# State sums copied by ScalarE, and rank and table products queued behind column transposes or state reads, in an attention and top-1 expert kernel

## Chip, cores and metric

The kernel runs on one core of one Trainium2 chip. The metric is the time of one execution on the device in microseconds (us); the number for a kernel is the median of several runs. Three runs of the kernel before gave 663.51, 663.2 and 663.98 us.

## What is computed

The reference is attention in both directions between tokens and states, followed by a layer of experts in which each row goes to one expert. Cut to what matters:

```python
# x: 8 batches, 8 heads, 512 tokens, 64;  state: 8, 8, 32, 64
scores = x @ state.T / 8                    # per batch and head
xread  = softmax(scores) @ state            # token reads, over the 32 states
sread  = softmax(scores.T) @ x              # state reads, over the 512 tokens
x = concat([xread, sread], axis=2) -> rows  # 8 * (512 + 32) = 4352 rows of 512
e_idx = argmax(x @ w_gate)                  # one of 8 experts for each row
out[row] = gate_w * sigmoid(x @ w_output_gate)[e] * (relu(x @ w1[e]) @ w2[e])
```

## The kernel before

The program has two stages. The first, some 185 us, is the attention and the routing; the second runs the experts in units of two or three tiles of 128 rows, under an order written by hand. The change lies wholly in the first stage, in whose code the order on each engine is set by a scheduler: it takes instructions in the order in which they are written, as far as their inputs and buffers are expected to be ready.

The first stage loops over the eight batches b (lines 468 to 499). What matters of one step, with its lines:

- `x_trans(b+1)`: TensorE transposes x (line 325), ScalarE copies to SBUF (327).
- `e2_trans(b)`: transposes of the column exponentials (424), copied by ScalarE (426).
- `scores(b+1)`: products (337), scaled by ScalarE into `s_sb` (340). VectorE takes the row maximum (344), subtracts it (346), ScalarE takes exp (347), VectorE sums and inverts (348 to 350), GpSimd multiplies (351).
- `a_trans(b)`: transposes of the row softmax of b (359); ScalarE writes the high half `aThi` (362), VectorE the low half `aTlo` (363).
- `columns_softmax(b+1)`: eight transposes of `s_sb` (401, the "column transposes"), VectorE's maximum (403), ScalarE's exp (406), VectorE's sum and inverse (407, 408).
- `state_reads(b)`: products of x and the column softmax into the single buffer `pss` (436, the "state reads"), and two copies of 64 by 256 out of it into `srT` (440, the "state sums").
- `token_reads(b)`: four groups px0 to px3 of six products each (380 to 382; 382 reads `aTlo`), each copied out by ScalarE (383).
- `state_out(b)` after b = 3 and b = 7: products of `srT` with the gate weights (449), read by VectorE (453 to 455).
- For GpSimd there are also the split of state values (205 to 210), the split of expert weights (496, 497), and small copies (415).

Routing runs beside this in generators that `go_on` advances. A route finds each row's expert (227 to 235 on VectorE), ranks the rows of each expert by products with a triangular matrix (243 to 247, the "rank products", also in `pss`), turns ranks to places (252 to 286), and builds for each chunk of 128 rows a pair `pa`, `rb` (294, 296), whose product is added to the table of row numbers `tid_ps` (300, the "table products"). `pa` has three buffers, and the scratch tile `lgp` of line 453 takes one of the same three.

Four limits set the order: TensorE, VectorE, ScalarE and GpSimd each execute their own list strictly as it stands; all large results of TensorE share three PSUM buffers named `psb` (transposes, scores, px groups, `state_out`); `pss` has one buffer; and each buffer is free only when its last reader is done.

After the loop, the rest of the routing ends in a chain of small VectorE operations and table products, twelve warm-up products (line 138, called at 503), the gathers of the first unit (614), its transposes (625), and the first expert products (655).

## Time and profile before

| what | value |
|---|---|
| runs of the kernel before | 663.51 us median, 663.2 to 663.98 |
| profiled execution | 662.72 us, span 661.0 us |
| TensorE matmul busy | 615.7 us, 93% of the span |
| VectorE, ScalarE, GpSimd busy | 283.8, 235.3, 181.8 us |
| first expert product starts | 188.91 us |
| mean granted TensorE clock | 0.968 |

The span is from the first to the last instruction; 1.72 us of the execution's time lie outside it. In a row of the timeline stand the start, the duration, the engine (PE is TensorE, DVE VectorE, ACT ScalarE, POOL GpSimd), the line of the kernel, the operation, output and inputs, the number of instructions merged and, in brackets, how long the engine sat idle before and whom that wait is put down to. The view of windows gives for each stretch its length, then for PE, PE's weight loads, DVE, ACT and POOL the busy time with the number of instructions, then the granted clock (1.00 is full), the share of the DMA engines and GB/s. A TensorE product of 32-bit data with 64 columns of output shows as two instructions.

### The profile page before, as it was taken

To read this page: it belongs to the slowest core of one execution; us is meant where nothing else is said; L and a number is where in the kernel's file an instruction comes from. 1 tells how busy PE (TensorE), PEld (TensorE's weight loads), DVE (VectorE), ACT (ScalarE), POOL (GpSimd) and SP (SyncE) were. 2 spreads that over 40 slices of the span, in tenths; PEclk is the share of its full clock that TensorE was granted. 3 is DMA by queue.
4 is the path that set the end of the run, shared out by engine and by line. 5 is a ranking of instruction groups with operands and counts; after the bars stand their busy time and mean duration, and the time that the engine had idled before them with its cause. 6 is when DMAs were issued, how large, how long until landed. Compare 5 with 4: busy or idle time off the path is not lost. (4 is left out here: it accounts for less than half of the span.)

```text
span 661.0 us, 11440 instructions
## 1 busy us (share of the span) xinstructions
PE 615.7 (93%) x3941; PEld 551.6 (83%) x3941; DVE 283.8 (43%) x626; ACT 235.3 (36%) x391; POOL 181.8 (27%) x286
## 2 busy tenths in 40 slices
PE   7989979998689999999999999999999999999990
PEld 4888978897468998998989989898898998988980
DVE  5547797878863211221235243154123424363210
ACT  3455534445042222222334244244233424462210
POOL 8154562641041221121122203124111220322210
PEclk8989998999679999999999999999999999999996
DMA  8533442323175220220146224325314522475200
GB/s 221 213 123 101 152 160 63 129 68 116 35 244 178 67 82 19 66 84 33 51 161 193 83 93 171 124 83 199 141 51 161 193 82 83 150 266 194 67 34 19
DMA packets 46288, 78.56 MB, mean 119 GB/s; under 512 B 11056, under 2 KB 19248, under 8 KB 46192
## 3 DMA queue, kind: packets, MB, share of 16 engines
q1 hardware_dynamic: 38592, 52.00, 24.1%
q0 software_dynamic: 7600, 25.38, 11.4%
q8 instruction: 49, 0.80, 0.5%
q14 instruction: 47, 0.39, 0.2%
HBM read 101.98 MB, written 19.42 MB: 184 GB/s over the span
## 5 line engine op out<-in xcount | busy, mean ns | idle before, releaser
L662 DVE SCALAR_TENSOR_TENSOR hlo<-p,hhi 128x256 fp32r<-128x256 f32 (+1 forms) x136 | 62.1, 462 | 226.9 <-ACT hhi L661 214.6
L655 PE MATMUL p<-xhi,whi 128*128 128x256 f32 (+1 forms) x544 | 151.2, 301 | 1.2 <-ACT xhi L627 0.8
L656 PE MATMUL p<-xhi,wlo 128*128 128x256 f32 (+1 forms) x544 | 150.1, 298 | 1.5 <-issue 1.5
L688 POOL DMA_INDIRECT out_dram<-y,idx x38 | 39.5, 1040 | 319.7 <-ACT y L687 236.0
L681 PE MATMUL po<-whi,hhi 128*128 128x512 f32 x304 | 122.6, 403 | 0.0
L682 PE MATMUL po<-wlo,hhi 128*128 128x512 f32 x304 | 120.1, 395 | 0.0
L655 PEld LDWEIGHTS p<-xhi,whi 128*128 128x128 f32 x544 | 103.6, 191 | 2.3 <-ACT rest_of L671 1.1
L661 ACT ACTIVATE hhi<-p 128x256 fp32r<-128x256 f32 (+1 forms) x136 | 56.5, 417 | 137.6 <-PE p L658 134.6
L656 PEld LDWEIGHTS p<-xhi,wlo 128*128 128x128 f32 x544 | 103.5, 190 | 1.9 <-issue 1.7
L658 PE MATMUL p<-xlo,whi 128*128 128x256 f32 (+1 forms) x544 | 95.9, 298 | 0.0
L685 PE MATMUL po<-whi,hlo 128*128 128x512 f32 x304 | 83.2, 395 | 0.0
L658 PEld LDWEIGHTS p<-xlo,whi 128*128 128x128 f32 x544 | 81.1, 190 | 0.0
L614 POOL DMA_INDIRECT xg<-xa,idx x57 | 66.2, 1161 | 48.7 <-issue 17.1
L687 ACT ACTIVATE y<-po,xg 128x512 f32<-128x512 f32 x38 | 26.2, 689 | 132.7 <-PE po L685 49.7
L685 PEld LDWEIGHTS po<-whi,hlo 128*128 128x128 f32 x304 | 57.0, 187 | 14.0
L682 PEld LDWEIGHTS po<-wlo,hhi 128*128 128x128 f32 x304 | 57.2, 188 | 11.6
L681 PEld LDWEIGHTS po<-whi,hhi 128*128 128x128 f32 x304 | 57.1, 188 | 11.5
L642 DVE TENSOR_TENSOR wlo<-stage,whi 128x2048 fp32r<-128x2048 f32 x24 | 54.3, 2285 | 11.6 <-ACT whi L635 11.6
L628 DVE TENSOR_TENSOR xlo<-pxT,xhi 128x512 fp32r<-128x512 f32 x39 | 25.9, 687 | 62.7 <-ACT xhi L627 62.7
L635 ACT CAST whi<-stage 128x2048 fp32r<-128x2048 f32 x24 | 45.1, 1901 | 3.8 <-DVE hlo L662 1.7
L627 ACT CAST xhi<-pxT 128x512 fp32r<-128x512 f32 x39 | 22.2, 583 | 30.7 <-PE pxT L625 30.7
L436 PE MATMUL pss<-e2T,xb 128*128 128x64 f32 x256 | 29.9, 275 | 1.1 <-ACT e2T L426 1.1
(190 smaller groups left out, 726.1 us busy)
## 6 DMA issues: line engine op xcount, KB each, us to landing
stage<-in_moe_w_dram SPq DMA_DIRECT2D x74, 1024.0 KB
xb<-in_x_dram SPq DMA_DIRECT2D x7, 1024.0 KB
xa<-xm SPq DMA_DIRECT2D x7, 1024.0 KB
xb<-in_x_dram SPq DMA_DIRECT2D x2, 512.0 KB
xa<-xm SPq DMA_DIRECT2D x4, 256.0 KB
xg<-xa,idx POOLq DMA_INDIRECT x57, 3.6
out_dram<-y,idx POOLq DMA_INDIRECT x38, 3.1
sraw<-in_state_dram SPq DMA_DIRECT2D x2, 256.0 KB
```

Source lines behind the costliest of these rows:

```text
L614: g = nc.gpsimd.indirect_dma_start(out=xg_all[u % 3][i], out_offset=None, in_=xa[:, :], in_offset=bass.IndirectOffsetOnAxis(ap=ix, axis=0))
L635: nc.scalar.copy(whi[i], stage[i])
L642: nc.vector.tensor_sub(wlo[i], stage[i], whi[i].bitcast(F32))
L655: nc.tensor.matmul(p1[:, :n], lhsT=whi[i][:, k, c], rhs=hi[:, k, :n], start=(k == 0), stop=False)
L656: nc.tensor.matmul(p1[:, :n], lhsT=wlo[i][:, k, c], rhs=hi[:, k, :n], start=False, stop=False)
L658: nc.tensor.matmul(p1[:, :n], lhsT=whi[i][:, k, c], rhs=lo[:, k, :n], start=False, stop=(k == KX - 1))
L661: nc.scalar.activation(hhi[:, fb, :n], p1[:, :n], AF.Relu)
L662: nc.vector.scalar_tensor_tensor(hlo[:, fb, :n], in0=p1[:, :n], scalar=0.0, in1=hhi[:, fb, :n].bitcast(F32), op0=ALU.max, op1=ALU.subtract)
L681: nc.tensor.matmul(po, lhsT=hhi[:, f, c], rhs=whi[j][:, k, :], start=(f == 0), stop=False)
L682: nc.tensor.matmul(po, lhsT=hhi[:, f, c], rhs=wlo[j][:, k, :], start=False, stop=False)
L685: nc.tensor.matmul(po, lhsT=hlo[:, f, c], rhs=whi[j][:, k, :], start=False, stop=(f == KH - 1))
L688: nc.gpsimd.indirect_dma_start(out=out[:, :], out_offset=bass.IndirectOffsetOnAxis(ap=idx[:, W * u + t : W * u + t + 1], axis=0), in_=y, i ...
```

## The change

Two things are changed. The two copies of the state sums (440) are issued on ScalarE instead of VectorE. And two kinds of products get an ordering edge, without a semaphore, to the latest column transpose or state read on the same engine (`st["pe"]`): the first rank product of a route, unless it is one of the last, and each table product while fewer than NT - 9 = 25 are done. Such an edge only tells the scheduler that the product may not stand before that instruction in TensorE's list.

```diff
+    def behind(inst, before):
+        tc.add_manual_dep(inst.ins, before.ins.name, mybir.DependencyInfo(mybir.DependencyClass.NoSync, mybir.DependencyReason.DATA), reason="order")
...
-            nc.tensor.matmul(rkv, lhsT=tri, rhs=ohb, start=True, stop=False)
+            m = nc.tensor.matmul(rkv, lhsT=tri, rhs=ohb, start=True, stop=False)
+            if len(done) < NT - 5:
+                behind(m, st["pe"])
...
                     done.append(nc.tensor.matmul(tid_ps, lhsT=pa, rhs=rb, ...
+                    if len(done) < NT - 9:
+                        behind(done[-1], st["pe"])
...
-                    nc.tensor.transpose(tp[:, g, P * c : P * c + P], s_v[:, c, g, :], ident)
+                    st["pe"] = nc.tensor.transpose(tp[:, g, P * c : P * c + P], s_v[:, c, g, :], ident)
...
-                    nc.tensor.matmul(srv[:, h], lhsT=xb[:, h, 2 * cc : 2 * cc + 2, :]...
+                    m = nc.tensor.matmul(srv[:, h], lhsT=xb[:, h, 2 * cc : 2 * cc + 2, :]...
+            st["pe"] = m
...
-                nc.vector.tensor_copy(srT[D * k : D * k + D, :, NS * bb : NS * bb + NS], srv[D * k : D * k + D, :, k, :])
+                nc.scalar.copy(srT[D * k : D * k + D, :, NS * bb : NS * bb + NS], srv[D * k : D * k + D, :, k, :])
```

The scheduler's lists differ at three kinds of places. Line numbers in the changed file are higher by 4 to 9: its 449 is the copy of line 440, 391 is 383, 355 is 347, 409 is 401, 247 to 253 are 243 to 247, and 371 is 363.

ScalarE at b = 2 (b = 6 reads alike), first before, then changed. `s_sb` are scores, `a_sb` the row exponentials, `e` the column exponentials, `xm` the copies of px groups:

```order
L340 ACTIVATE s_sb<-psb 128x1024
L362 CAST aThi<-psb 128x1024
L347 ACTIVATE a_sb<-a_sb 128x1024
L383 COPY xm<-psb 128x544
L406 ACTIVATE e_790,st_788<-psb,st_788 128x512 x2
```

```order
L348 ACTIVATE s_sb<-psb 128x1024
L370 CAST aThi<-psb 128x1024
L449 COPY srT<-pss 64x8x32 x2
L355 ACTIVATE a_sb<-a_sb 128x1024
L391 COPY xm<-psb 128x544
L414 ACTIVATE e_790,st_788<-psb,st_788 128x512 x2
```

The copies stand between the high half and the row exponential, so the exponential, the px copies and the column exponential queue behind the state reads.

VectorE from b = 3 to b = 4, first before, then changed (`lgp` and `xs` are what `state_out` reads from PSUM, `st_1184` the row statistics of the next scores):

```order
L294 TENSOR_SCALAR pa<-iota_q,rf_1004 128x128
L296 TENSOR_SCALAR rb<-iota_q,sm_861,vid 128x272
L453 TENSOR_TENSOR lgp<-psb,rs 128x128
L455 TENSOR_TENSOR xs<-psb,rs 128x512
L454 TENSOR_REDUCE lgt<-lgp 128x16
L294 TENSOR_SCALAR pa<-iota_q,rf_1004 128x128
L227 TENSOR_REDUCE sm_1106<-lgt 128x1
```

```order
L302 TENSOR_SCALAR rb<-iota_q,sm_861,vid 128x272
L352 TENSOR_REDUCE st_1184<-s_sb 128x32
L371 TENSOR_TENSOR aTlo<-psb,aThi 128x1024
L462 TENSOR_TENSOR lgp<-psb,rs 128x128
L464 TENSOR_TENSOR xs<-psb,rs 128x512
L463 TENSOR_REDUCE lgt<-lgp 128x16
L354 TENSOR_TENSOR a_sb<-s_sb,st_1184 128x1024
L231 TENSOR_REDUCE sm_1106<-lgt 128x1
```

The three reads of `state_out` moved behind the next batch's row maximum and low half: the table products that free `lgp`'s buffer are now held behind the column transposes.

TensorE at b = 1 (b = 3 and b = 5 are of the same kind), first before, then changed:

```order
L245 MATMUL pss<-ohb_477,ones 128x8
L247 LDWEIGHTS ones
L247 MATMUL pss<-run_bf,ones 128x32
L401 MATMUL psb<-ident,s_sb 128x128 x8
L380 MATMUL psb<-sbd_181,aThi 128x272
L381 MATMUL psb<-sbd_182,aThi 128x272
```

```order
L367 MATMUL psb<-ident,a_sb 128x128 x8
L409 MATMUL psb<-ident,s_sb 128x128 x8
L247 LDWEIGHTS tri
L247 MATMUL pss<-ohb_477,tri 128x32
L251 LDWEIGHTS ones
```

The rank products moved from ahead of the column transposes to behind them. At b = 2 and b = 6 two table products moved in the same way, and two state reads stand in their place. At b = 7 the changed list has the rank products ahead of all token reads, where before they stood among them, and VectorE makes their input ahead of the low half, not behind it. On GpSimd two small value splits (209, 210) moved ahead of a multiplication; on SyncE the small write of line 458 moved ahead of the last load of x, and one row write of b = 7 behind two factor writes.

## Prediction

> **What bounds the kernel now.** I read the page, then the timeline of each engine from 28 us to 200 us, then the view of windows. A change within 0.2% of the run, some 1.3 us, is about what a measurement of this kernel cannot tell from none.

> ```profile
> span 661.0 us, 11440 instructions
> ...
> PE 615.7 (93%) x3941; PEld 551.6 (83%) x3941; DVE 283.8 (43%) x626; ACT 235.3 (36%) x391; POOL 181.8 (27%) x286
> ```

> TensorE bounds the kernel. Its work is the same after the change, so time can come only from its idle stretches in the attention stage and from its clock. For the clock I cut the timeline where the granted clock jumps, and the jumps lie on a grid of 3.41 us:

> ```profile
> 37.79:41.20 3.41, 1.07 (x7) 0.85 (x8) 2.90 (x5) 1.45 (x4) 1.91 (x1) 1.00 0.74 244
> 41.20:44.61 3.41, 3.41 (x18) 3.41 (x17) 0.13 (x1) 1.74 (x3) 0.72 (x4) 0.50 0.01 3
> 95.83:99.24 3.41, 1.34 (x13) 1.23 (x12) 3.35 (x8) 0.00 (x0) 3.15 (x8) 1.00 1.01 302
> 99.24:102.65 3.41, 3.41 (x19) 3.41 (x18) 2.90 (x3) 0.25 (x1) 3.27 (x5) 0.50 0.78 213
> 157.24:160.65 3.41, 2.14 (x22) 1.84 (x22) 3.04 (x13) 0.77 (x2) 0.00 (x0) 1.00 0.26 94
> 167.48:170.89 3.41, 1.69 (x20) 1.59 (x18) 2.43 (x11) 0.00 (x0) 0.00 (x0) 1.00 0.01 2
> 187.96:191.37 3.41, 2.66 (x13) 2.47 (x12) 2.62 (x11) 2.49 (x2) 0.00 (x0) 0.50 0.84 308
> 191.37:194.78 3.41, 3.41 (x18) 3.41 (x17) 0.42 (x1) 0.73 (x2) 2.72 (x3) 0.50 1.06 392
> 194.78:198.20 3.42, 3.42 (x31) 3.42 (x30) 3.01 (x3) 2.15 (x4) 2.81 (x3) 1.00 0.73 234
> ```

> A window with PE busy 1.07 or 1.34 us is followed by one at half clock. So idle time is charged twice: as itself, and as a window at half speed. Between 50% busy (1.69 us) and 63% (2.14 us, and I found no half clock behind it) lies the threshold. Back to full clock 78% (2.66) was not enough, 100% was.

> The idle stretch of b = 0 is the first that the copies of line 440 make:

> ```profile
> 35.41 0.86 DVE L440 COPY srT<-pss 64x256 f32<-64x256 f32 x2 [2.00 <-PE pss L436]
> 36.45 1.04 PE L401 MATMUL psb<-ident,s_sb 128*128 128x128 f32 x8
> 38.16 1.23 DVE L403 TENSOR_REDUCE st<-psb 128x2 f32<-128x1024 f32 x1
> 39.30 1.22 DVE L363 TENSOR_TENSOR aTlo<-psb,aThi 128x1024 fp32r<-128x1024 f32 x1
> 40.57 0.40 PE L382 MATMUL psb<-sbd,aTlo 128*128 128x272 f32 x1 [2.34 <-DVE aTlo L363]
> ```

> **The change part by part. The copies at b = 0.** VectorE waited 2.00 us for the state reads, with line 348 queued behind the copies. Without them line 348 starts 2 us earlier and line 403 waits only for the transposes, done at 36.45 + 1.04 = 37.49: it starts at 37.55 instead of 38.16, and so does everything to line 382. Gain 0.6; bounds 0 and 2.2, the upper one if the half-clock window behind it goes too. I keep that window, since 1.07 + 0.6 = 1.67 us busy is still about the 1.69 that was followed by half clock.

> **The rank products held, at b = 1, 3 and 5**, are worth nothing:

> ```profile
> 51.29 1.03 ACT L340 ACTIVATE s_sb<-psb 128x1024 f32<-128x1024 f32 x1 [2.42 <-PE psb L337]
> 52.37 1.09 PE L401 MATMUL psb<-ident,s_sb 128*128 128x128 f32 x8
> 54.82 0.39 PE L382 MATMUL psb<-sbd,aTlo 128*128 128x272 f32 x1 [1.03 <-DVE aTlo L363]
> ```

> The transposes need `s_sb`, which ends at 52.32; they start at 52.37 with or without rank products ahead. The products, some 0.4 us, filled that gap; now they stand in front of line 380, where the 1.03 us wait for `aTlo` hides them. If that cover went, they would cost 0.4 each.

> **The copies at b = 2.** A copy of 256 columns out of PSUM on ScalarE I take from its nearest row, a Relu:

> ```profile
> 191.87 0.38 ACT L661 ACTIVATE hhi<-p 128x256 fp32r<-128x256 f32 x1 [0.71 <-PE p L658]
> 73.48 1.06 ACT L347 ACTIVATE a_sb<-a_sb 128x1024 f32<-128x1024 f32 x1 [2.88 <-DVE a_sb L346]
> 74.27 0.37 PE L380 MATMUL psb<-sbd,aThi 128*128 128x272 f32 x1
> 75.31 0.61 ACT L383 COPY xm<-psb 128x544 f32<-128x544 f32 x1 [0.78 <-PE psb L382]
> ```

> Two copies take some 0.68 us as their starts overlap (between 0.5 and the 1.22 of two rows of line 383). They wait for the state reads, whose successor on TensorE starts at 74.27; in the new list two reads fill the wait for `s_sb`, so they end 0.2 earlier, and complete at some 74.3. The exponential behind the copies then starts at 74.9 instead of 73.48, 1.4 later; 0.78 idle before line 383 and 0.1 of overlap absorb part. The first px copy comes 0.55 later, and so do the column exponentials; px2 and px3 need their PSUM buffers. TensorE, which did not wait on ScalarE here, loses 0.55 (0 to 1.4). Queued behind the copies are lines 347, 383 and 406; VectorE's 348 waits for the first.

> **The copies at b = 3** are the gain:

> ```profile
> 92.20 3.79 PE L436 MATMUL pss<-e2T,xb 128*128 128x64 f32 x32
> 94.84 1.98 DVE L294 TENSOR_SCALAR pa<-iota_q,rf 128x128 fp32r<-128x128 f32 x1
> 97.48 0.43 DVE L440 COPY srT<-pss 64x256 f32<-64x256 f32 x1
> 98.05 2.60 PE L449 MATMUL psb<-idw,srT 128*128 128x80 f32 x16 [2.07 <-DVE srT L440]
> 100.45 2.99 PE L325 MATMUL psb<-ident,xb 128*128 128x128 f32 x16
> 137.33 1.92 PE L325 MATMUL psb<-ident,xb 128*128 128x128 f32 x16
> 167.07 1.98 PE L449 MATMUL psb<-idw,srT 128*128 128x80 f32 x16 [0.72 <-DVE srT L440]
> ```

> The reads end at 95.99, but the copies stood behind a stretched `pa` (1.98 us) and ended at 97.91. ScalarE has nothing to do there, so line 449 can start some 0.8 behind the reads: 0.68 for the copies and a hand-over of at most 0.14, as from 97.91 to 98.05. Of the 2.07, 1.3 go (bounds 0.7, with copies at 1.22, and 1.5). The gain of b = 0 and the loss of b = 2 nearly cancel, so the grid lies as before against this place. Its window then holds 77% work and is not followed by half clock: lines 449 and 325 fall from 2.60 + 2.99 to 1.98 + 1.92, less the 0.1 that an end overlaps: another -1.55 (bounds -1.7 and 0, if that window is not at half clock in the usual run).

> [...]

> **The table products held, at b = 4.**

> ```profile
> 103.67 0.29 DVE L453 TENSOR_TENSOR lgp<-psb,rs 128x128 f32<-128x128 f32 x1 [1.54 <-PE tid_ps L300]
> 103.88 0.68 DVE L455 TENSOR_TENSOR xs<-psb,rs 128x512 f32<-128x512 f32 x1
> 104.48 0.36 DVE L454 TENSOR_REDUCE lgt<-lgp 128x16 f32<-128x128 f32 x1
> 116.11 0.33 PE L325 MATMUL psb<-ident,xb 128*128 128x128 f32 x1 [0.34 <-ACT e L406]
> ```

> Already before, line 453 waited for table products. Now these stand behind the transposes of b = 4, and lines 453, 455 and 454 behind `aTlo`. Two costs: `state_out` keeps one of three PSUM buffers through the step, so px0 starts only with `aTlo`; and the three operations, 1.1 us with their overlap, delay line 403 and with it line 406, for which the next x transposes (116.11) already wait. State reads filled that gap; they stand later now. I charge the 1.1, and 0.2 for two products of px0 that used to run ahead of `aTlo` (each 0.4 in the row of line 382, half of it overlapped): 1.3 (0 to 1.8).

> **The copies at b = 6** repeat b = 2, but route work is in the way:

> ```profile
> 151.84 1.92 POOL L351 TENSOR_TENSOR a_sb<-a_sb,st 128x1024 f32<-128x1024 f32 x1 [10.77 <-DVE st L350]
> 152.33 1.45 DVE L407 TENSOR_SCALAR st<-st 128x2 f32<-128x2 f32 x1 [0.64 <-ACT e L406]
> 154.48 0.41 DVE L296 TENSOR_SCALAR rb<-iota_q,sm,vid 128x272 fp32r<-128x272 f32 x1
> 159.30 0.39 PE L382 MATMUL psb<-sbd,aTlo 128*128 128x272 f32 x1 [0.69 <-DVE aTlo L363]
> ```

> While GpSimd ran line 351 (to 153.76), a tiny VectorE operation issued at 152.33 ended only at 153.78: such operations wait out line 351. That line follows the exponential and moves 1.4 later, to 153.3 and, behind an `rb` that comes first, 155.4. Only then come `pa` and `rb` of the sixth table product, 0.7 together: 156.1 instead of 154.89, 1.2 later. Behind that product TensorE queues the rest of line 424, the transposes 359 and the rank products. VectorE passes the delay on: the two copies, 0.85, leave its list, and four operations for the rank input, about as much, come ahead of `aTlo`. I take 1.3 for line 382, less 0.25 for rank products that stood behind it: +1.05 including the 0.55 (0.3 to 1.6). TensorE idles 0.6 before px3 and 1.7 for the sixth product, 1.9 of it in one window of 3.41, which is over the threshold; half clock may then fall on token reads: +0.5, as a half of 1.0 (0 to 1.7).

> **The tail.**

> ```profile
> 165.96 0.42 DVE L440 COPY srT<-pss 64x256 f32<-64x256 f32 x1 [1.31 <-PE pss L436]
> ```

> VectorE did another operation between the two copies, and line 449 (167.07) came 1.1 behind the reads; with 0.8 as above it gains 0.35, say 0.4 (0 to 0.5). The moved writes on SyncE and splits on GpSimd are due a step later: nothing.

> **Sum:** -0.6 + 0.55 - 1.3 - 1.55 + 1.3 + 1.05 + 0.5 - 0.4 = -0.45. The profiled execution took 662.72 (661.0 and 1.72 outside the span), so it would take 662.3; it lies 0.79 under the median of the runs shown, and against that median, 663.51, the forecast is 663.1.

> **The rivals.** *The grid pays out.* If the half clock stays away at b = 6, the tail starts 0.95 early. Then the first expert window (187.96) holds all of its 3.41 us of work instead of 2.66, and the clock rises one window sooner. Half of 3.41 us at half clock, 1.7, is saved, less half of the shift, 0.5: -0.95 - 1.2 = -2.15, so 661.4. It decides from a shift of between 0 and 0.75 us, which the threshold between 78% and 100% leaves open. Against: it needs the same grid in each run. [...]

> *ScalarE's queue costs more than it frees.* b = 2 costs its bound, 1.4 instead of 0.55, and at b = 6 the clock falls and the next window, with waits in it, stays below what lifts it: two windows at half, 1.7 instead of 0.5. That is -0.45 + 0.85 + 1.2 = +1.6, so 665.1. It decides from 1.7 us idle in one window at b = 6. For it: my own count gives 1.9. Against: part of the half-speed work lies under waits.

> *It does nothing:* idle time only changes its names, and the half-clock window of b = 3 moves elsewhere: 663.5.

> **How the numbers follow.** Forecast 0.43, its own range 662.2 to 664.4; the grid 0.33; ScalarE's queue 0.18; nothing 0.06. Faster by over 0.2% (under 662.2): 0.31 of the grid and 0.02 of the forecast, 0.33. Slower (over 664.8): 0.14 and 0.03, 0.17. Within: 0.50. The range 661.0 to 664.9 takes in two thirds of the grid case and half of the slow one, in all about 0.8; the bounds of b = 0 and b = 4 below lie inside the grid's case.

> **What would show it.** Right: line 449 at b = 3 starts 0.8 behind the reads and no half-clock window follows; line 347 at b = 2 and 6 starts 1.4 later after the copies; px0 at b = 4 waits for `aTlo`; table products at b = 6 wait for `rb` about 1.9 us. Wrong: the exponential is not late, the gate opens or shuts at other places, or the expert stage itself changes length after its first 10 us.

## The result, and the profile after

The changed kernel took 671.66 us, the median of four runs (669.24 to 673.98), against 663.36 us, the median of four runs of the kernel before on the same chip: a ratio of 1.0125, 95% interval 1.0087 to 1.0163. The forecast was 663.1, with a range up to 664.9. Three executions of 1025 to 1540 us, two of the kernel before and one of the copies alone, are left out of the ratios and ranges below. The profiled execution took 672.15 us, its span was 670.5 us, and the first expert product started at 199.49 instead of 188.91 us. So 10.6 us were lost before the experts began, and the expert stage was 1.1 us shorter.

The head of the page after shows 8 us more of busy TensorE at the same number of products. That is work at half clock: the mean granted clock was 0.953 instead of 0.968, and between 28 and 204 us fourteen windows of 3.41 us ran at half clock, before eight:

```profile
span 670.5 us, 11438 instructions
...
PE 623.7 (93%) x3941; PEld 559.9 (84%) x3941; DVE 277.3 (41%) x610; ACT 240.9 (36%) x407; POOL 183.8 (27%) x286
```

Three of the forecast places first. In the timeline after, b = 2 (ScalarE's copies, the exponential behind them, px2 of token reads) and b = 3 (state reads, `state_out`, and the x transposes behind it):

```profile
76.87 0.75 ACT L449 COPY srT<-pss 64x256 f32<-64x256 f32 x2 [3.70 <-PE pss L444]
77.64 1.06 ACT L355 ACTIVATE a_sb<-a_sb 128x1024 f32<-128x1024 f32 x1
...
79.39 0.39 PE L388 MATMUL psb<-sbd,aThi 128*128 128x272 f32 x1 [1.00 <-ACT xm L391]
...
95.34 3.79 PE L444 MATMUL pss<-e2T,xb 128*128 128x64 f32 x32
99.96 2.01 PE L458 MATMUL psb<-idw,srT 128*128 128x80 f32 x16 [0.83 <-ACT srT L449]
101.81 1.91 PE L333 MATMUL psb<-ident,xb 128*128 128x128 f32 x16
```

At b = 2 the exponential stands behind the copies and px2 waits 1.00 us. At b = 3 the products of `state_out` start 0.83 us behind the reads, not 2.07, and run at full clock, in 2.01 us, not 2.60, as does line 333, in 1.91, not 2.99. All that was forecast.

Up to here the changed kernel was 1.9 us late (line 458 at 99.96, line 449 before at 98.05). At the state reads of b = 1 it had been 2.6 us late (61.25, before 58.68), which the windows of b = 0 explain; b = 2 added 0.6, and b = 3 took back 1.2. The columns of these windows are length, PE, its weight loads, VectorE, ScalarE and GpSimd with numbers of instructions, then the granted clock. First after, then one row of before:

```profile
30.81:34.22 3.41, 2.70 (x24) 2.71 (x25) 2.55 (x5) 1.71 (x2) 0.74 (x1) 1.00 0.00 0
34.22:37.63 3.41, 3.41 (x18) 3.41 (x18) 1.73 (x3) 0.73 (x2) 2.64 (x2) 0.50 0.09 18
37.63:41.05 3.42, 2.40 (x12) 2.08 (x10) 1.43 (x2) 1.12 (x2) 0.45 (x1) 0.50 0.92 289
44.46:47.87 3.41, 3.41 (x17) 3.41 (x17) 0.00 (x0) 1.67 (x3) 0.78 (x4) 0.50 0.00 0
```

```profile
30.96:34.37 3.41, 2.78 (x25) 2.78 (x25) 2.45 (x4) 1.64 (x2) 0.81 (x1) 1.00 0.00 0
```

The half clock began one window earlier, at 34.2, though the state reads started within 0.1 us of those before (31.52 and 31.59): the window behind which it fell lay 0.15 us earlier. It lasted four windows instead of one.

Since line 333 ran at full clock, the e2 transposes behind it (line 432) started only 0.4 us late, at 103.95 instead of 103.53. The state reads of b = 5 started 10.2 us late, at 143.92 instead of 133.71. So the loss lies in b = 4. The timeline after, TensorE, then VectorE with GpSimd's line 359:

```profile
110.62 0.62 PE L306 MATMUL tid_ps<-rb,pa 128*128 128x272 f32 x3
...
112.22 0.39 PE L388 MATMUL psb<-sbd,aThi 128*128 128x272 f32 x1 [0.99 <-DVE aTlo L371]
...
116.20 1.09 PE L333 MATMUL psb<-ident,xb 128*128 128x128 f32 x8 [0.44 <-ACT xm L391]
117.54 0.87 PE L333 MATMUL psb<-ident,xb 128*128 128x128 f32 x6 [0.26 <-ACT e L414]
118.86 0.17 PE L247 MATMUL pss<-ohb,tri 128*128 128x8 bf16 x1 [0.44 <-DVE ohb L239]
...
122.02 6.25 PE L444 MATMUL pss<-e2T,xb 128*128 128x64 f32 x32 [1.65 <-DVE t L265]
...
110.95 1.22 DVE L371 TENSOR_TENSOR aTlo<-psb,aThi 128x1024 fp32r<-128x1024 f32 x1
112.08 0.28 DVE L462 TENSOR_TENSOR lgp<-psb,rs 128x128 f32<-128x128 f32 x1
...
118.45 0.36 DVE L239 CAST ohb<-oh 128x8 bf16<-128x8 f32 x1
...
120.02 1.87 DVE L261 TENSOR_TENSOR run_sb<-run_sb,oh 128x8 f32<-128x8 f32 x1
121.81 0.15 DVE L265 TENSOR_TENSOR t<-oh,pss 128x8 f32<-128x8 f32 x1
...
119.90 1.96 POOL L359 TENSOR_TENSOR a_sb<-a_sb,st 128x1024 f32<-128x1024 f32 x1
```

The chain reads from the top of VectorE's rows. `lgp` (line 462) started at 112.08, before at 103.67. Its buffer is freed by table products that now stand behind the column transposes (line 306 at 110.62), so the scheduler put the three reads of `state_out` behind `aTlo` (line 371). So the one-hot rows of that route came at 118.45, the rank products into `pss` at 118.86, and the read that frees `pss` (line 265) at 121.81, held up once more by the small sum of line 261, which took 1.87 us (0.16 in the kernel before) and ended within 0.03 us of GpSimd's line 359. The state reads need `pss` and stood 1.65 us. In the kernel before, the one-hot rows came 12 us earlier and the small sum was long done. The read of `pss` ended 0.2 us ahead of the state reads (116.73), which waited for nothing:

```profile
106.42 0.17 DVE L235 CAST ohb<-oh 128x8 bf16<-128x8 f32 x1
...
116.39 0.15 DVE L259 TENSOR_TENSOR t<-oh,pss 128x8 f32<-128x8 f32 x1
...
116.73 3.68 PE L436 MATMUL pss<-e2T,xb 128*128 128x64 f32 x32
```

What the wait brought, in the windows after:

```profile
119.55:122.97 3.42, 1.77 (x17) 1.64 (x15) 3.39 (x16) 1.04 (x2) 3.09 (x8) 1.00 0.73 270
122.97:126.38 3.41, 3.41 (x19) 3.41 (x18) 2.34 (x7) 0.00 (x0) 3.41 (x4) 0.50 0.01 2
129.79:133.21 3.42, 3.42 (x18) 3.42 (x18) 2.13 (x11) 0.29 (x1) 0.00 (x0) 0.50 0.91 286
136.62:140.03 3.41, 3.41 (x25) 3.29 (x24) 2.95 (x3) 1.01 (x1) 0.00 (x0) 0.50 0.00 0
140.03:143.45 3.42, 2.98 (x22) 2.59 (x22) 2.65 (x3) 2.61 (x5) 0.00 (x0) 1.00 0.00 0
```

One window at 52% is followed by five at half clock (122.97 to 140.03), with TensorE busy for all 3.41 us of each. Line 444 takes 6.25 us instead of the 3.68 of line 436 before.

### The profile page after: what moved, and what is told of

It is laid out like the page before. It is cut to its first block, busy times and chain, and to the rows that moved or that the text cites. A ratio compares the mean times of both kernels' runs of the same rounds, so it can differ in the third digit from the quotient of the medians.

```text
span 670.5 us, 11438 instructions
## 1 busy us (share of the span) xinstructions
PE 623.7 (93%) x3941; PEld 559.9 (84%) x3941; DVE 277.3 (41%) x610; ACT 240.9 (36%) x407; POOL 183.8 (27%) x286
## 5 line engine op out<-in xcount | busy, mean ns | idle before, releaser
L623 POOL DMA_INDIRECT xg<-xa,idx x57 | 68.0, 1193 | 49.4 <-issue 18.0
L444 PE MATMUL pss<-e2T,xb 128*128 128x64 f32 x256 | 33.5, 293 | 2.8 <-DVE t L265 1.6
L444 PEld LDWEIGHTS pss<-e2T,xb 128*128 128x128 f32 x256 | 32.6, 209 | 3.6 <-DVE t L265 2.1
```

Of the source, the lines that this page charges most:

```text
L444: m = nc.tensor.matmul(srv[:, h], lhsT=xb[:, h, 2 * cc : 2 * cc + 2, :].rearrange("p c d -> p (c d)"), rhs=e2T[:, 2 * cc : 2 * cc + 2, NS ...
L623: g = nc.gpsimd.indirect_dma_start(out=xg_all[u % 3][i], out_offset=None, in_=xa[:, :], in_offset=bass.IndirectOffsetOnAxis(ap=ix, axis=0))
```

## Experiments

Theory A: the held table products cost the time, by way of `lgp`'s buffer, the route of `state_out`, the single `pss` and the clock. Theory B: ScalarE's copies cost it. Medians are of several runs; each ratio is to the kernel before on the same chip, with its 95% interval. The experiments ran on four chips, on which the kernel before took 663.55 to 664.13 us, so a difference of two medians can hold some 0.5 us of that.

**Parts of the change.** The copies without the holds:

```diff
-                behind(m, st["pe"])
-                        behind(done[-1], st["pe"])
```

> The state sums are copied by ScalarE, and no product is held. Theory A (the held table products cost the time: the three reads of state_out wait at b = 4 for a buffer of pa, its route comes late, and the state reads of b = 4 wait for the single pss buffer, which brings half clock): without the holds the state reads of b = 4 start with no wait for VectorE's line 265, no half clock follows between 115 and 145 us, and the time is 662 to 664, or up to 666 if the longer half clock of b = 0 (34 to 48 us in the changed kernel) stays. Theory B (the copies in ScalarE's queue cost the time): 669 or more, with a half-clock stretch of several windows at b = 4.

663.15 us, 0.9996 (0.9976 to 1.0016). Theory B is out. There was no half clock from 104 to 170 us. One row and the windows of b = 3 in this kernel show what the forecast had not seen:

```profile
96.38 0.57 PE L306 MATMUL tid_ps<-rb,pa 128*128 128x272 f32 x1 [1.29 <-DVE rb L302]
```

```profile
93.04:96.45 3.41, 2.12 (x20) 1.98 (x19) 3.41 (x11) 0.73 (x2) 3.16 (x7) 1.00 0.78 276
96.45:99.86 3.41, 3.41 (x16) 3.41 (x17) 2.38 (x6) 0.00 (x0) 3.23 (x6) 0.50 1.01 309
99.86:103.28 3.42, 3.42 (x18) 3.42 (x18) 2.36 (x12) 1.01 (x1) 2.23 (x5) 0.50 0.36 57
```

Without the hold, a table product stands ahead of line 458 and waits 1.29 us for `rb`: most of the gap is back. The copies pay at b = 3 only together with the held table products.

The holds without the copies:

```diff
-                nc.scalar.copy(srT[D * k : D * k + D, ...
+                nc.vector.tensor_copy(srT[D * k : D * k + D, ...
```

> Both kinds of products are held, but VectorE copies the state sums as before. Theory A: 669 to 673, the state reads of b = 4 wait over 1 us for VectorE's line 265, and four or more half-clock windows follow. Theory B: 663 to 664. At b = 0 VectorE's copies are back, so if the copies made the longer half clock there, it is one window from 41 us again.

671.41 us, 1.0113 (1.0082 to 1.0143): the whole loss. In its timeline the wait is the same:

```profile
121.79 5.81 PE L444 MATMUL pss<-e2T,xb 128*128 128x64 f32 x32 [1.65 <-DVE t L265]
```

In this execution the half-clock windows of b = 0 and b = 3 lay as in the trace of before (41.31 and 99.33), and line 458 started at 98.02, so the loss can be read cleanly: the state reads of b = 5 start at 143.32 instead of 133.71, 9.6 us later. Four half-clock windows (123.23 to 136.88) hold back some 4 x 3.41 / 2 = 6.8, an estimate, since work at half clock takes about twice as long (line 367 in the changed kernel took 1.92 us at 135.14 and 1.04 at 53.67). The rest is nearly all waits: from line 458 to there TensorE stood idle for 5.4 us, in the kernel before for 2.8.

Copies and the table hold, without the rank hold:

```diff
-                behind(m, st["pe"])
```

> ScalarE copies and held table products, without the hold of the rank products. Theory A: the rank products are worth nothing, so 669 to 674 as the changed kernel. If the rank hold is what makes pss late, 664 to 666.

671.83 us, 1.0119 (1.0089 to 1.0148), beside 671.66 with the rank hold: that hold shows no worth here, within intervals some 4 to 5 us wide.

**The links of the chain.** `lgp` in a buffer that nobody else needs by then:

```diff
-                lgp = asm.tile([P, NG, 4, GC], F32, name="lgp", tag="pa", bufs=3)
+                lgp = asm.tile([P, NG, 4, GC], F32, name="lgp", tag="pal", bufs=5)
```

> The whole change, but the scratch tile lgp takes a buffer of the tag pal, which is free until the end of the stage, instead of one of the three of pa. Theory A: the reads of state_out no longer wait for table products, the rank products of its route come before the px groups, pss is free in time and no half clock follows: 662 to 666. If it is the held products themselves that TensorE waits for (and not lgp's buffer), or Theory B: 669 or more.

661.13 us, 0.9957 (0.9938 to 0.9976): not only is the loss gone, it is faster than before, and than the 662 to 666 expected. Its timeline at the places of the chain:

```profile
101.41 0.28 DVE L462 TENSOR_TENSOR lgp<-psb,rs 128x128 f32<-128x128 f32 x1
...
109.78 0.18 PE L247 MATMUL pss<-ohb,tri 128*128 128x8 bf16 x1
...
117.31 3.79 PE L444 MATMUL pss<-e2T,xb 128*128 128x64 f32 x32 [0.42 <-DVE t L265]
```

All products are held as in the changed kernel. Only the buffer differs, and the order that the scheduler makes of it: `lgp` is written 10.7 us earlier, and the rank products come 9.1 us earlier.

The wait filled with work: the eight transposes of line 432 that stand ahead of the state reads of b = 4 (they belong to b = 5, hence the 5 in the code) are issued three times, and the first state read is ordered behind the last of them.

```diff
-            for g in range(NG):
+            for g in list(range(NG)) * (3 if b == 5 else 1):
```

> The whole change, and the eight transposes of line 432 that stand before the state reads of b = 4 are issued three times over (they write the same values): 16 more, at 0.104 us each some 1.66 us of TensorE work, which fit into the 1.65 us that the state reads wait for pss. Theory A with the clock gate (of the 10 us lost at b = 4, some 7 are half-speed work behind one idle window): the state reads start at the same place, but at full clock, no half-clock window follows between 119 and 140 us, and the time is 663.5 to 667, although TensorE does more work. If the waits themselves are the loss: 671 to 674, or 1.7 more.

663.53 us, 0.9998 (0.9983 to 1.0012): 8.1 us less than the changed kernel, with 1.7 us more of work (2.78 less the 1.04 of eight). A timeline row for the 24 transposes, the state reads, which start at once behind them, and the window that holds both:

```profile
116.58 2.78 PE L432 MATMUL psb<-ident,e 128*128 128x128 f32 x24
119.44 3.79 PE L446 MATMUL pss<-e2T,xb 128*128 128x64 f32 x32
```

```profile
119.06:122.47 3.41, 3.33 (x30) 3.09 (x29) 3.35 (x20) 0.21 (x1) 3.16 (x8) 1.00 0.10 36
```

VectorE read `pss` as late as ever, at 119.24, some 3 us behind the rank products, so the wait is not shorter, it is only filled; and no half clock follows. All twelve runs took 665.35 us or less, all four of the changed kernel 669.24 or more. This shows the clock as the larger part of the loss. (The profiled execution also had no half clock at b = 0, where that of the changed kernel had four windows; what part of the 8.1 this is in the medians was not measured.)

The last link, the small sum that took 1.87 us beside GpSimd's line 359:

```diff
+            t0 = asm.tile([P, nch, E], F32, name=f"t0{nch}", tag="t0")
+            nc.vector.tensor_tensor(t0, oh, rkv, op=ALU.mult)
             if nch > 1:
                 add = ...
...
-            t0 = asm.tile([P, nch, E], F32, name=f"t0{nch}", tag="t0")
-            nc.vector.tensor_tensor(t0, oh, rkv, op=ALU.mult)
```

> The whole change, but VectorE reads the ranks out of pss (the product of line 265) ahead of the running sums (lines 257 to 262). In the changed kernel that read came behind the sum of line 261, which took 1.87 us while GpSimd ran line 359. If only the sum waits for GpSimd, the read runs some 1.8 us earlier, the state reads of b = 4 start at about 120.4 without waiting, no half clock follows, and the time is 663.5 to 667. If a small operation in that place waits for GpSimd whichever it is, the read takes the 1.9 us itself, and the time is 669 to 674 as the changed kernel.

661.44 us, 0.9976 (0.9962 to 0.9991), below the 663.5 to 667 expected. In its timeline the read of `pss` is now line 257 and the sum line 263:

```profile
119.75 0.15 DVE L257 TENSOR_TENSOR t<-oh,pss 128x8 f32<-128x8 f32 x1
119.82 1.80 DVE L263 TENSOR_TENSOR run_sb<-run_sb,oh 128x8 f32<-128x8 f32 x1
...
119.63 1.97 POOL L359 TENSOR_TENSOR a_sb<-a_sb,st 128x1024 f32<-128x1024 f32 x1
...
119.95 3.79 PE L444 MATMUL pss<-e2T,xb 128*128 128x64 f32 x32
```

The read took 0.15 us beside GpSimd's line 359, the sum behind it 1.80, and the state reads did not wait. Exchanging two instructions of 128 by 8 numbers is worth some 10 us here.

**What the parts are worth once the chain is broken.** `lgp` apart in the kernel before, with nothing of the change:

```diff
-                lgp = asm.tile([P, NG, 4, GC], F32, name="lgp", tag="pa", bufs=3)
+                lgp = asm.tile([P, NG, 4, GC], F32, name="lgp", tag="pal", bufs=5)
```

> The kernel before, with nothing of the change, but lgp in a buffer of pal. Tells whether the 2.5 us that the change with lgp apart gains on the kernel before come from lgp alone. Theory A1 (lgp's buffer matters only where table products are held, since before they came early): 663 to 664. Theory A2 (the wait of 1.54 us before line 453 cost time before as well): 661 to 662.

665.34 us, 1.0022 (1.0005 to 1.0039): A2 is out, and A1's figure was missed by a small loss, whose cause was not sought. (In the profiled execution it is 0.9 us at the state reads of b = 5, 1.5 at the first expert product and 4.0 at the end.) So the gain of the kernel with `lgp` apart comes from the change.

Both holds and `lgp` apart, copies on VectorE:

```diff
-                nc.scalar.copy(srT[...
+                nc.vector.tensor_copy(srT[...
...
-                lgp = ... tag="pa", bufs=3)
+                lgp = ... tag="pal", bufs=5)
```

> Both holds and lgp apart, but VectorE copies the state sums as before. The difference to the change with lgp apart (661.1) is what ScalarE's copies are worth there. By the prediction's terms, without those of the table products, the copies are worth 0.6 + 1.3 + 1.55 + 0.4 - 0.55 less 0.5 to 1 at b = 6, some 2 to 2.5: 663 to 664. If the grid decides whether the gap of b = 3 costs a half-clock window, the difference is under 1.5: 661.5 to 662.5.

668.38 us, 1.0062 (1.0043 to 1.0081), a miss for both readings: beside the kernel with `lgp` apart, ScalarE's copies are worth 7.2 us by the medians, which are from two chips, and 7.0 by the ratios. In the two profiled executions, which had the same half clock at b = 0, the kernel without them is behind by 2.1 us at the state reads of b = 4 (119.43 to 117.31), 3.6 at those of b = 7, 5.3 at the first expert product and 6.2 at the end. It has two half-clock windows that the other has not, at 100.87 behind the 2.08 us gap of b = 3, and at 162.31.

The copies and `lgp` apart, nothing held:

```diff
-                behind(m, st["pe"])
...
-                        behind(done[-1], st["pe"])
...
-                lgp = ... tag="pa", bufs=3)
+                lgp = ... tag="pal", bufs=5)
```

> ScalarE's copies and lgp apart, no product held. Tells what the holds are worth once lgp is apart (with them 661.1). If they are worth nothing: 661 to 662. If they make the gain: 663 to 664, as the copies alone (663.15).

662.7 us, 0.9982 (0.996 to 1.0004), between the two expectations: of the 2.8 us that the change with `lgp` apart gains on the kernel before, 1.2 is left without the holds, with an interval that takes in none. The row of the table product at 96.38 fits that.

The copies of b = 2 and b = 6 back on VectorE, `lgp` apart:

```diff
-                nc.scalar.copy(srT[...
+                (nc.vector.tensor_copy if b in (2, 6) else nc.scalar.copy)(srT[...
```

> The change with lgp apart, but the copies of b = 2 and b = 6 stay on VectorE. By the prediction's terms ScalarE's copies cost 0.55 at b = 2 and 1.05 at b = 6 with half a window of clock, 0.5: 659 to 660 instead of 661.1. px2 of b = 2, which waits 1.00 us for the px copy in the changed kernel, should not wait. If VectorE's copies cost as much in another place there (the kernel with holds, lgp apart and all copies on VectorE took 668.4): 661 to 664.

659.96 us, 0.995 (0.9925 to 0.9974). From the state reads of b = 2 to those of b = 3 it takes 22.66 us, with ScalarE's copies 23.46; from b = 6 to b = 7 17.75 and 18.41. So the copies cost 0.80 and 0.66 there. The medians differ by 1.2, but the ratios' intervals overlap.

`lgp` apart and the early read of `pss`, and then the copies of b = 2 and b = 6 on VectorE as well:

```diff
+            nc.vector.tensor_tensor(t0, oh, rkv, op=ALU.mult)
             if nch > 1:
...
-            nc.vector.tensor_tensor(t0, oh, rkv, op=ALU.mult)
...
-                lgp = ... tag="pa", bufs=3)
+                lgp = ... tag="pal", bufs=5)
```

> The whole change with both remedies: lgp in a buffer of pal, and VectorE's read of pss ahead of the running sums. With lgp apart the state reads of b = 4 still waited 0.42 us for that read. If the two gains add where they can: 660 to 661. If they mend the same loss and no other: 661 to 662, the 661.1 of lgp apart and the 661.4 of the early read again.

660.24 us, 0.9938 (0.9918 to 0.9957). With the third edit:

```diff
-                nc.scalar.copy(srT[...
+                (nc.vector.tensor_copy if b in (2, 6) else nc.scalar.copy)(srT[...
```

> The whole change with lgp in a buffer of pal, the read of pss ahead of the running sums, and the copies of b = 2 and b = 6 on VectorE. Each of the last two alone took the kernel with lgp apart from 661.1 to 660.2 and 660.0, in measurements of about 1 us of spread. If the two are independent, as they stand at different steps: 659 to 660. If both only moved the median by chance: 660.5 to 662.

659.27 us, 0.9937 (0.9914 to 0.996), the fastest median. By the ratios both are some 4 us faster than the kernel before, and by the medians 11 to 12 faster than the changed one; between the two the ratios tell no difference.

**The grid.** Where the clock jumped to half, in the profiled execution of each kernel, between 28 and 170 us. Within an execution the jumps lie whole multiples of 3.413 us apart (in the changed kernel 34.23 to 47.88 is four of them, 34.23 to 122.97 twenty-six); the phase is a jump's time modulo 3.413.

| kernel | phase | half clock, us |
|---|---|---|
| before | 0.24 | 41.20-44.61, 99.23-102.65 |
| changed | 0.09 | 34.23-47.88, 122.97-140.03 |
| copies alone | 0.87 | 96.45-103.28 |
| holds alone | 0.35 | 41.31-44.72, 99.33-102.75, 123.23-136.88 |
| copies and table | 2.37 | 33.09-39.92, 43.33-46.74, 121.83-138.90 |
| lgp apart | 2.44 | 33.16-39.99, 43.40-46.81 |
| wait filled | 1.30 | 96.87-100.28 |
| pss read first | 3.27 | 33.99-47.64 |
| before, lgp apart | 1.22 | 42.18-45.59, 100.20-103.61 |
| holds, lgp apart | 1.88 | 32.60-39.43, 42.84-46.25, 100.87-104.28, 162.31-165.72 |
| lgp apart, pss first | 0.33 | 41.29-44.70 |
| lgp apart, VectorE at 2, 6 | 0.25 | 41.21-44.62 |
| copies, lgp apart | 1.77 | 97.34-100.75 |
| all three | 1.22 | 154.83-158.24 |

The phase is another one in nearly every execution. At b = 0 the five executions with a window that ends between 32.60 and 34.23 have the early half clock, one of them with the copies on VectorE; the nine others have not. So the longer half clock of the changed kernel's profile there goes by the phase and is chance, not the change. Behind 170 us each execution has four to six more half-clock windows up to 204 us, and five of the fourteen have one more at 453 to 463 us, so one execution alone says little on a gain of 2 us.

## Why the prediction was wrong, step by step

**The step that failed** is "The table products held, at b = 4", +1.3 with bounds 0 and 1.8. It had the right cause: the three reads of `state_out` late by `pa`'s buffer, and px0 waiting for `aTlo`, as came out (0.99 us). It followed that lateness along VectorE to line 406 and along the PSUM buffer to px0, but not along the data: `lgt` feeds a route, the route's rank products take the single `pss`, and the next user of `pss` are the very state reads of which it says that they "stand later now". The description of the kernel lists `pss` among its four limits, and this step priced no wait for it. The waits measured 2.6 us (5.4 idle less 2.8, holds alone) instead of 1.3. The other omission was larger: it looked for windows under the threshold at b = 0, b = 3 and b = 6 and never counted idle time at b = 4. The window there fell to 1.77 us (1.76 in holds alone), close to the 1.69 quoted as too little, and cost 6.8 us in four windows (holds alone).

**What a half-clock window costs.** The prediction priced one window each time, with 1.55 or 0.5. At b = 4 it took four or five, all with TensorE busy throughout. "Back to full clock 78% (2.66) was not enough, 100% was" holds for the rows that it quoted, which are px groups, products of `state_out` with transposes, and expert products, and not for those of b = 4. Its threshold, between 1.69 and 2.14 us busy, does not hold in general either: 2.70 us (30.81 to 34.22 in the changed kernel) was followed by half clock.

**The same grid in each run** was assumed for every clock term. The table shows otherwise, with phases between 0.09 and 3.27 us, and the 22 runs of the kernel before, taken beside the first four experiments, lie between 660.86 and 666.11 us, where the first three lay within 0.8. The prediction named this as the weak point of its rival "the grid pays out" only.

**The copies at b = 0**, -0.6: with the copies alone the wait for `aTlo` there fell from 2.34 to 1.70 us. Right; what the clock makes of it goes by the phase. The prediction kept the half-clock window behind it; four executions with the copies on ScalarE, at phases from 0.87 to 1.77, had none at b = 0, and the one with VectorE's copies in that range (before with `lgp` apart, 1.22) had it. So the case of its upper bound, this window gone, occurs too.

**The rank holds**, 0: nothing measured speaks against it, within the intervals of copies and table.

**The copies at b = 2 and b = 6**, +0.55 and +1.05: they measured 0.80 and 0.66, within the bounds, each in one pair of executions (0.79 for b = 2 in a second pair, with the early read of `pss`). At b = 6 a table product of the changed kernel waited 1.13 us for `rb`, where 1.7 to 1.9 were forecast. The further 0.5 for half clock at b = 6 did not come: no execution with the copies of b = 6 on ScalarE had a half-clock window there. The rival "ScalarE's queue costs more than it frees" gave the right sign for a reason that did not occur.

**The copies at b = 3**, -1.3 and -1.55: from the state reads to line 458 it took 4.62 us instead of 5.85, -1.23. With the copies and the table hold, one of eight executions (the filled wait) had a half-clock window there; with the copies on VectorE, four of four. So mechanism and size were right, but the gain was credited to the copies alone, and needs the table hold beside them.

**The tail**, -0.4: from the state reads of b = 7 to line 458 4.51 us instead of 4.83, -0.3.

Had the chain been seen, the other terms gave the sign: the change with that one buffer moved gained 2.8 us of 663.9. What stays open is the size of the whole: the copies were worth some 7 us beside holds and `lgp` apart, far more than the terms, and single profiled executions at different phases don't divide that among them.

## What to carry to other kernels

When a reader of a buffer gets later, follow its data to the last consumer, through every single-buffered tile on the way, until an instruction of the bounding engine stands behind it. Price idle time on TensorE by its windows: a wait of 1.65 us cost four to five half-speed windows here, so that a tile with a buffer of its own, a different order of two tiny instructions, or useless products in the gap were each worth 8 to 10.5 us. And take clock terms from several executions, since the grid lies differently in each.

## What the runs showed of the hardware that was not expected

While GpSimd ran line 359, VectorE's sum of two 128 by 8 tiles in SBUF took 1.87 us in the changed kernel (line 261; 0.16 in the kernel before, line 255 at 106.50, with GpSimd idle), and the product of one such tile with `pss` 0.15 us in the kernel that reads `pss` first (line 257). Both started 0.12 us behind line 359. What makes the difference was not measured. So the prediction's remark at b = 6, that tiny VectorE operations wait out GpSimd's multiplication, drawn from the 1.45 us of line 407, is too wide.
